# No plain pair of blocks in the first layer, the first half of tile 2's x kept only in sums, and other rules for the order of the work

## The chip, the cores and the metric

The kernel runs on one core of a Trainium2 chip: TensorE (PE) multiplies, VectorE (DVE), ScalarE (ACT) and GpSimd (POOL) do the elementwise work, SyncE (SP) issues the loads and stores. The metric is the device time of one execution in microseconds. Before the change the median of three runs is 571.93 (569.59 to 574.9).

## The reference

Linear attention with decay runs over 2 batches, 8 heads, 768 positions and 64 columns per head; its output, 1536 tokens of 512 columns, goes through two MLP layers of 2048 hidden columns.

```python
for b in range(nb):                        # blocks of 64 positions
    intra = einsum('bhic,bhjc->bhij', qb, kb) * Dmask
    out[:, :, sl] = einsum('bhij,bhjd->bhid', intra, vb) + einsum('bhid,bhde->bhie', qb * lam_pow, kv_state)
    kv_state = lam_block * kv_state + einsum('bhsd,bhse->bhde', kb * rev_pow, vb)
x = out.transpose(0, 2, 1, 3).reshape(1536, 512)
h = x @ w_in;  g = where(h > 0, h, exp(min(h, 0)) - 1);          x = g @ w_out      # layer 0
h = x @ w_in2; g = maximum(h, 0) + log1p(exp(-abs(h)));        out = g @ w_out2     # layer 1
```

## The kernel before

**Attention** goes in 12 chunks of 128 positions, 6 for each batch (`attention_ops`). A chunk has on PE the scores (tile `sps`, 16 small matmuls), the state (`stps`, not in the last chunk of a batch) and the mixing (`xps`: 16 matmuls with the state, L245, which the first chunk of a batch lacks, and 16 with the masked scores, L250). VectorE masks the scores (`sc`, L235), adds the state (L288), writes the low part of x (`xl`, L271). q is scaled by `qpow` (L211), k by `kdecay` (L219) and the state faded (L293) on POOL or VectorE. ScalarE writes the high part of x (`xh`, L267). q and k of a chunk come in one load (`qk`), k and v in another (`kv`), 512 KB each. From chunk 6 on `kv` has two buffers, so chunk 8's load waits for the mixing of chunk 6, and so on.

**The MLP.** Tokens form three tiles of 512 (t = 0, 1, 2; four chunks each), hidden columns 16 blocks of 128 for each layer. Each factor is kept as a high and a low part, so each 128 x 128 piece of a product takes three matmuls of 512 columns (L303 to L305). The first product of one tile and one block, x @ w_in (tile `hps`), has twelve; so has the second one, g @ w_out (tiles `y0` to `y3`, L353, a quarter each), which adds into `y` over four or more blocks. Between them stand ScalarE's and VectorE's activation and the split of g into two parts. Weights come packed (`raw`); two ScalarE passes, two VectorE passes, a ScalarE copy and a VectorE subtraction make the parts (`wih`, `wil`, `woh`, `wol`). There are two `raw` buffers, so a weight load waits until ScalarE has read the one before last.

**The plan** (`plan`) names the first products in order: `one` is tile 0 with one block; `two` is tiles 1 and 2 with a pair of blocks, four plain products of twelve matmuls (48); `fast` does the same pair with seven half products of six matmuls (42), from sums of x pieces (t1 to t4, `first_sums`) and sums of weight pieces (`sumsw`, `s0h` to `s1l`, `sum_ops`). With x11 and x12 for the first 256 columns of x in tiles 1 and 2, and x21 and x22 for the last 256, t1 = x12 - x11, t2 = x22 - t1, t3 = x22 - x12, t4 = x21 - t2. Before the change layer 0 has eight `one`, a `two`, three `fast`, and then groups of four `one` and two `fast`; layer 1 has only such groups.

**The order.** At build time `schedule` walks through the work with assumed durations and writes each engine's instructions into a fixed order, which the chip then follows; an engine waits where its next instruction isn't ready. An operation has a key (its due time) and those it waits for. For PE it chooses between attention, the next first product and the next second product: a second product is taken when no first product is ready, or when those that are ready pile up to `PILE` products (L444). POOL gets an operation only when VectorE has `QUEUE` of them ready. `FIRST_LOADS` sets the order of the first loads on SP.

Of the kernel before, what the change touches and what calls it, by code (L numbers as in the profile page):

```python
# [9 lines left out]
F32 = mybir.dt.float32  # L10
# [23 lines left out]
FAST = (True, True)  # L34

# [5 lines left out]
def plan():  # L41
    p = [("one", 0, c) for c in range(EARLY)]
    p += [("two", 0, 0)] + [("fast" if FAST[0] else "two", 0, q) for q in range(1, 4)]
    for b in (2, 3):
        p += [("one", 0, c) for c in range(4 * b, 4 * b + 4)]
        p += [("fast" if FAST[0] else "two", 0, q) for q in (2 * b, 2 * b + 1)]
    for b in range(4):
        p += [("one", 1, c) for c in range(4 * b, 4 * b + 4)]
        p += [("fast" if FAST[1] else "two", 1, q) for q in (2 * b, 2 * b + 1)]
    return p  # L50
# [5 lines left out]
def body(ctx, tc, lamc, attqk, attkv, w1, w2, out):  # L56
# [27 lines left out]
    def new_x(t, layer):  # L84
        for parts, k in ((xh, "h"), (xl, "l")):
# [170 lines left out]
    def att_parts(g):  # L256
# [134 lines left out]
    def schedule(pe, free):  # L391
# [8 lines left out]
        def enter(op):  # L400
            for e in op.on:
                if e != "P":
# [3 lines left out]
        def begin(op, e):  # L406
# [8 lines left out]
            if e == "S" and took[0] == "dma":  # L415
                wire[0] = max(now + LATENCY, wire[0]) + took[1]
# [4 lines left out]
            heappush(events, (now + late + 0.12, next(seen), op))  # L421
# [5 lines left out]
        while left:  # L427
# [11 lines left out]
            if free["P"] <= now:  # L439
# [4 lines left out]
                if can[0] and (not can[1] or sum(o.on["P"][0] for o in ahead) / (4 * MM3) >= PILE and not m1_seq[heads[1]].first):  # L444
# [29 lines left out]
    FIRST, STEP, ATT = 21.0, 7.0, 3.95  # L474
    SHIFT = 6
# [3 lines left out]
    FIRST_LOADS = [("q", 0), ("v", 0), ("q", 1), ("v", 1), ("q", 2), ("v", 2), ("q", 3), ("v", 3), 0, ("q", 4), ("v", 4), 1, ("q", 5), ("v", 5), ("q", 6)]  # L479
# [13 lines left out]
    def build():  # L493
# [22 lines left out]
        for kind, layer, c in PLAN:  # L516
# [3 lines left out]
            elif kind == "two":  # L520
                for i, t in PAIR:
                    stand((layer, t, 2 * c + i), 4 * MM3)
                    made[layer, t, 2 * c + i] = at_[0] + 4.0
# [28 lines left out]
        def weights_ops():  # L552
            for k, task in enumerate(tasks):
                key = want(task) - 3.0
# [3 lines left out]
                ld = Op({"S": ("dma", 1.28)}, lkey(k, key), w_load, [loads[t2][1] if t2 else None], lambda k=k: loaded[0] == k)  # L558
# [69 lines left out]
        att_seq, closed = [], []  # L628

        def attention_ops():  # L630
# [3 lines left out]
            ramp = Op({"V": (1.36, False)}, chunk_at(0) + 2.0, powers, [spin])  # L634
# [10 lines left out]
            for g in range(NCHUNK):  # L645
# [29 lines left out]
                O["SC", g, 0] = Op({"V": PS_V}, k + 1.2, lambda g=g: att_sc(g, 0), [s, spin, O.get(("X", g - 2))])  # L675
                O["SC", g, 1] = sc1 = Op({"V": PS_V}, k + 1.3, lambda g=g: att_sc(g, 1), [O["SC", g, 0]], end=gave(g))

                if not last:
# [9 lines left out]
                    if g % CPB < CPB - 2:  # L688
                        O["FD", g] = Either(F_ON, k + 2.5, lambda e, g=g: att_fade(e, g), [ad, O.get(("AD", g - 1)), ramp])
# [7 lines left out]
                homes = []  # L697
# [651 lines left out]
```

## Time and profile before

| | us |
|---|---|
| median of 3 runs | 571.93 |
| the profiled execution | 572.88 |
| its span, first to last instruction | 571.2 |
| PE busy in the span | 555.7 |
| VectorE busy | 497.8 |
| ScalarE busy | 390.4 |
| POOL busy | 14.4 |

The span is what the trace covers; the profiled execution's own time has 1.7 us more. A row of a timeline gives when an instruction starts, how long it takes and, in brackets, how long its engine had been idle and what ended that. Durations of neighbours overlap a little (an operation on VectorE of 0.68 is followed by the next after 0.60), so prices are read from start to start. The granted clock is TensorE's, as a share of its full 2.4 GHz.

### The profile page before, as it was taken

Reading aid. Unit: us, or ns where it says so; the run is one execution under the profiler, and the core shown is the slowest. Engines: PE = TensorE matmul, PEld = TensorE weight load, DVE = VectorE, ACT = ScalarE, POOL = GpSimd, SP = SyncE. Lnnn points to the kernel's source line nnn. Section 1 sums busy time; section 2 is a strip of 40 time slices with the busy share of each in tenths; the row PEclk is TensorE's granted clock in tenths of the full one; section 3 lists DMA queues with packets and bytes.
Section 4 is the critical chain, followed back from the end, with each engine's and each line's share of the span. In section 5 each row is a group of like instructions: output and inputs, shape, how many; then the busy total and the mean of one; then the engine's idle time right before and its main releaser. Section 6 shows DMA issues by size and latency. Waiting matters only on the chain.

```text
span 571.2 us, 7940 instructions
## 1 busy us (share of the span) xinstructions
PE 555.7 (97%) x2933; PEld 458.0 (80%) x2933; DVE 497.8 (87%) x883; ACT 390.4 (68%) x699; POOL 14.4 (3%) x18
## 2 busy tenths in 40 slices
PE   8798899999999999999999999999999999999997
PEld 7687678888887888888888887888888888888885
DVE  7988789998958499876898999999999999986883
ACT  1376558566765678635878669997999678965550
POOL 1201210000000000000000000000000000000000
PEclk9899799999999999999999999999999999999999
DMA  8955643002014033300233001221122321000023
GB/s 318 405 199 189 242 162 112 0 1 73 2 46 140 26 111 113 127 30 1 73 111 111 1 1 38 73 75 55 56 75 75 109 72 42 1 0 0 2 92 130
DMA packets 14583, 49.80 MB, mean 87 GB/s; under 512 B 1745, under 2 KB 1745, under 8 KB 14545
## 3 DMA queue, kind: packets, MB, share of 16 engines
q1 hardware_dynamic: 14544, 49.30, 25.2%
q8 instruction: 23, 0.38, 0.3%
q14 instruction: 16, 0.12, 0.1%
HBM read 46.14 MB, written 3.15 MB: 86 GB/s over the span
## 4 chain that ended last, share of the span: by engine, by line
PE 89%; DMA 5%; DVE 3%; SPq 1%; ACT 1%; issue 1%; POOL 0%; POOLq 0%; DVEq 0%; ACTq 0%
PE y L353 44%; PE hps L303 6%; PE hps L304 6%; PE hps L305 6%; PE pa L304 5%; PE pa L303 5%; PE pa L305 5%; DMA raw<-w 3%; PE pd L303 2%; PE pd L304 2%; PE pd L305 2%; DMA kv<-attkv 2%; PE xps L250 2%; PE xps L245 1%; PE pb L303 1%; PE pb L304 1%
## 5 line engine op out<-in xcount | busy, mean ns | idle before, releaser
L353 PE MATMUL y<-woh,g 128*128 128x512 f32 x384 | 118.7, 390 | 1.1 <-DVE g L485 0.7
L353 PE MATMUL y<-g,woh 128*128 128x512 f32 x384 | 118.8, 390 | 0.0
L802 ACT ACTIVATE g<-v 128x512 fp32r<-128x512 f32 x96 | 60.4, 629 | 52.2 <-PE y L353 47.6
L485 DVE TENSOR_TENSOR g<-v,g 128x512 fp32r<-128x512 f32 x96 | 65.7, 686 | 22.7 <-ACT g L802 22.2
L353 PEld LDWEIGHTS y<-woh,g 128*128 128x128 f32 x384 | 72.1, 188 | 16.7 <-DVE g L485 1.0
L353 PEld LDWEIGHTS y<-g,woh 128*128 128x128 f32 x384 | 71.8, 188 | 15.2
L353 PE MATMUL y<-g,wol 128*128 128x512 f32 x192 | 74.7, 389 | 0.0
L353 PE MATMUL y<-wol,g 128*128 128x512 f32 x192 | 74.7, 389 | 0.0
L303 PE MATMUL hps<-xh,wih 128*128 128x512 f32 x136 | 53.7, 395 | 1.8 <-DVE xl2b L271 1.1
L304 PE MATMUL hps<-xl,wih 128*128 128x512 f32 x136 | 53.2, 391 | 0.0
L305 PE MATMUL hps<-xh,wil 128*128 128x512 f32 x136 | 53.0, 390 | 0.0
L564 ACT ACTIVATE r<-raw 128x512 f32<-128x512 f32 x64 | 42.7, 668 | 13.9 <-DMA raw<-w 9.3
L1121 DVE TENSOR_TENSOR yacc<-y,yacc 128x512 f32<-128x512 f32 x68 | 45.4, 688 | 5.8 <-PE y L353 5.4
L578 DVE CUSTOM_DVE_ANT_0 r<-r,c 128x1024 uint16<-128x1024 uint16 x64 | 45.2, 707 | 2.0 <-ACT c L568 1.0
L568 ACT ACTIVATE c<-raw 128x512 uint32<-128x512 uint32 x64 | 42.4, 663 | 0.1
L353 PEld LDWEIGHTS y<-g,wol 128*128 128x128 f32 x192 | 36.0, 188 | 7.5
L353 PEld LDWEIGHTS y<-wol,g 128*128 128x128 f32 x192 | 36.0, 188 | 7.5
L783 DVE SCALAR_TENSOR_TENSOR u<-u,e 128x512 f32<-128x512 f32 x48 | 32.8, 685 | 5.0 <-ACT v L779 5.0
L485 DVE TENSOR_TENSOR v<-v,u 128x512 f32<-128x512 f32 x48 | 32.9, 685 | 0.2
L303 PEld LDWEIGHTS hps<-xh,wih 128*128 128x128 f32 x136 | 25.7, 189 | 8.0 <-issue 1.4
L573 DVE TENSOR_SCALAR r<-r 128x512 uint32<-128x512 uint32 x64 | 27.3, 427 | 5.3 <-ACT r L564 5.3
L363 ACT ACTIVATE e<-e 128x512 f32<-128x512 f32 x48 | 30.0, 624 | 0.4
(187 smaller groups left out, 1103.9 us busy)
## 6 DMA issues: line engine op xcount, KB each, us to landing
raw<-w SPq DMA_DIRECT2D x64, 512.0 KB, 3.7
qk<-attqk SPq DMA_DIRECT2D x8, 512.0 KB, 7.1
kv<-attkv SPq DMA_DIRECT2D x8, 512.0 KB, 5.5
out<-yacc SPq DMA_DIRECT2D x12, 256.0 KB, 2.1
early<-attkv SPq DMA_DIRECT2D x2, 512.0 KB, 9.4
early<-attqk SPq DMA_DIRECT2D x2, 512.0 KB, 10.8
earlykv<-attkv SPq DMA_DIRECT2D x2, 512.0 KB, 11.2
earlyqk<-attqk SPq DMA_DIRECT2D x2, 512.0 KB, 11.1
```

What stands on the lines that cost most here:

```text
L303: T.matmul(ps, wh[:, wo[i]], xa[i], start=(start and i == 0), stop=False, skip_group_check=True)
L304: T.matmul(ps, wh[:, wo[i]], xb[i], start=False, stop=False, skip_group_check=True)
L305: T.matmul(ps, wl[:, wo[i]], xa[i], start=False, stop=(stop and i == n - 1), skip_group_check=True)
L353: T.matmul(yps[m], a, b, start=(begins(key) and i == 0), stop=(ends(key) and i == 2))
L363: A.activation(out=o, in_=a, func=AF.Exp, scale=-1.0)
L485: engines[e].tensor_tensor(out=o, in0=a, in1=b, op=ALU.subtract)
L564: A.activation(out=r, in_=high.bitcast(F32), func=AF.Prelu, scale=2.0 ** -112, alpha=-2.0 ** 32)
L568: A.activation(out=box["c"], in_=box["low"], func=AF.Copy, scale=2.0 ** -29)
L578: V.tensor_tensor(out=ri, in0=ri, in1=box["c"], op=ALU.add)
L783: V.scalar_tensor_tensor(out=u, in0=u, scalar=-1.0, in1=box["e"], op0=ALU.add, op1=ALU.subtract)
L802: A.activation(out=g[:, 0], in_=box["v"], func=AF.Copy)
L1121: V.tensor_tensor(out=y, in0=yps[m], in1=y, op=ALU.add)
```

## The change

The pair of blocks 0 and 1 of layer 0 becomes `fast` like the others. With it the split form of x12 has no user but the sums: the split tiles of tile 2 hold only the last 256 columns of x, and `att_copy` writes the mixing's result of chunks 8 to 11 once more as fp32 into a tile that lies in the place of `yacc0` (`x2`). `first_sums` works on that copy in place: t3 = x22 - x12 first, then t1, t2 and t4, with 12 adds for 20, and with no wait for the end of attention except for t3's parts.

In `schedule` second products are held during attention (`HELD`, 7.9 products, until attention's buffers are closed), after it they pile up to 2.4; POOL takes work when VectorE has two operations ready; weights get a due time 0.16 ahead of their use where it was 3.0; a load is assumed to land later (`LATE`) and results to be seen sooner (`MARGIN`); chunks 6 and 7 use the early PSUM banks (`SHIFT`); for chunks 0 to 7 q is scaled on VectorE alone; the keys of the attention steps and the order of the first loads are others (q 2, q 3, then v 2, v 3, q 4, and two weights ahead of v 4).

```diff
 def plan():
     p = [("one", 0, c) for c in range(EARLY)]
-    p += [("two", 0, 0)] + [("fast" if FAST[0] else "two", 0, q) for q in range(1, 4)]
+    p += [("fast", 0, q) for q in range(4)]
...
 def new_x(t, layer):
...
-                parts[t] = [
-                    None if layer and FAST[1] and i == "a" else
-                    xp.tile([P, 2, TT], F32R, tag=f"x{k}2{i}", name=f"x{k}2{i}") for i in "ab"
-                ]
+                parts[t] = None, xp.tile([P, 2, TT], F32R, tag=f"x{k}2b", name=f"x{k}2b")
...
 def att_parts(g):
-        return [(xps[g][:, 2 * i:2 * i + 2], xh[t][i][:, :, o], xl[t][i][:, :, o]) for i in range(2)]
+        return [(xps[g][:, 2:4], xh[t][1][:, :, o], xl[t][1][:, :, o])]
...
+    def att_copy(g, y):
+        o = slice(g % 4 * P, g % 4 * P + P)
+        A.activation(out=y[:, :, o], in_=xps[g], func=AF.Copy)
...
 def schedule(pe, free):
...
-                if can[0] and (not can[1] or sum(o.on["P"][0] for o in ahead) / (4 * MM3) >= PILE and not m1_seq[heads[1]].first):
+                if can[0] and (not can[1] or sum(o.on["P"][0] for o in ahead) / (4 * MM3) >= (PILE if late else HELD) and not m1_seq[heads[1]].first):
...
-    PILE, QUEUE = 1.9, 3
+    PILE, HELD, QUEUE = 2.4, 7.9, 2
...
+    KT, LATE, RAW_LAG, MARGIN = 3.0, 3.42, 0.28, 0.05
...
-                key = want(task) - 3.0
+                key = want(task) - KW
...
+                    O["XC", g] = Op({"A": SCALAR}, k + KX, copy, [xh_, O.get(("XC", g - 1))])
...
-        def first_sums(plain_end):
+        def first_sums():
...
+            box = held["x2"]
+            made = [attend["XC", g] for g in range(8, NCHUNK)]
...
+            def sub(key, fn, out_, a, b, deps):
+                return Either(T_SUM, key, lambda e: fn(e, out_(), a(), b()), deps)
...
+            def y(n, k):
+                return box["x2"][:, 2 * n + k]
...
             for k in range(2):
-                t1 = chain(("f1", k), at_[1], [start_],
-                           (minus, lambda k=k: x(2, 0, k)[0], lambda k=k: x(1, 0, k)[0]),
-                           (plus, None, lambda k=k: x(2, 0, k)[1]),
-                           (minus, None, lambda k=k: x(1, 0, k)[1]))
...
+                def new3(e, k=k):
+                    if "f3" not in box:
+                        box["f3"] = xp.tile([P, 2, TT], F32, tag="xh2a", name="f3")
+                    minus(e, box["f3"][:, k], y(1, k), y(0, k))
+
+                ya, yb, fc = lambda k=k: y(0, k), lambda k=k: y(1, k), lambda k=k: box["f3"][:, k]
+                f3 = Either(T_SUM, at_[3] - 3.0, new3, made + early_q)
+                f1 = sub(at_[1], minus, ya, ya, lambda k=k: x(1, 0, k, 0), [f3] + x1)
+                f1 = sub(at_[1], minus, ya, ya, lambda k=k: x(1, 0, k, 1), [f1])
+                f2 = sub(at_[2], minus, yb, yb, ya, [f1])
...
+                f4 = sub(at_[4], minus, ya, lambda k=k: x(1, 1, k, 0), yb, [f2, l1])
+                f4 = sub(at_[4], plus, ya, ya, lambda k=k: x(1, 1, k, 1), [f4])
...
-            elif kind == "two":
-                first = not any(k == "two" and l == layer and x < c for k, l, x in PLAN)
...
```


What this moves is seen at three places of the order.

**Place 1: VectorE at start-up**, up to the low part of chunk 3's x, on which the first MLP product waits (`sc`: masked scores, `r`, `c` and `wil`: a weight's conversion, `kv`, `early`: a k that is scaled or a q). Before:

```order
L485 TENSOR_TENSOR wil0_351<-r_301,wih0_328 128x512
L235 TENSOR_TENSOR sc_367<-sps0_313,dmask_96 128x512
L288 TENSOR_TENSOR state_371<-stps_330,faded_308 128x256
L235 TENSOR_TENSOR sc_367<-sps1_314,dmask_96 128x512
L235 TENSOR_TENSOR sc_376<-sps0_341,dmask_96 128x512
L573 TENSOR_SCALAR r_353<-r_353 128x512
L235 TENSOR_TENSOR sc_376<-sps1_342,dmask_96 128x512
L578 ISA r_353<-r_353,c_355 128x1024
L219 TENSOR_TENSOR kv_224<-kv_224,kdecay_97 128x512
L288 TENSOR_TENSOR state_418<-stps_357,faded_374 128x256
L485 TENSOR_TENSOR wil1_421<-r_353,wih1_416 128x512
L271 TENSOR_TENSOR xl0_227<-xps_378,xh0_226 128x4x128
```

Now:

```order
L287 TENSOR_TENSOR state_295<-stps_270,faded_264 128x256
L230 TENSOR_TENSOR sc_314<-sps0_282,dmask_96 128x512
L206 TENSOR_TENSOR early_139<-early_139,qpow_98 128x512
L230 TENSOR_TENSOR sc_314<-sps1_283,dmask_96 128x512
L574 TENSOR_SCALAR r_316<-r_316 128x512
L574 TENSOR_SCALAR r_324<-r_324 128x512
L579 ISA r_316<-r_316,c_321 128x1024
L270 TENSOR_TENSOR xl0_212<-xps_297,xh0_211 128x4x128
L287 TENSOR_TENSOR state_364<-stps_328,faded_318 128x256
L490 TENSOR_TENSOR wil0_368<-r_316,wih0_362 128x512
L579 ISA r_324<-r_324,c_366 128x1024
L270 TENSOR_TENSOR xl0_212<-xps_342,xh0_211 128x4x128
```

Ahead of the fourth `xl` stand the masked scores of chunks 0 to 3 now and of 0 to 4 before; two weights are converted together, and the scalings of two k's have left VectorE.

**Place 2: SP and PE in the middle of attention.** On SP (`kv_609`, `kv_696` and now `kv_569`, `kv_663` are the k and v of chunks 8 and 9). Before:

```order
L138 DMA raw_476<-w1 128x512
L138 DMA raw_509<-w1 128x512
L138 DMA raw_541<-w1 128x512
L138 DMA raw_579<-w1 128x512
L206 DMA kv_609<-attkv 128x1024
L138 DMA raw_634<-w1 128x512
L138 DMA raw_692<-w1 128x512
L206 DMA kv_696<-attkv 128x1024
L196 DMA qk_701<-attqk 128x1024
```

Now:

```order
L133 DMA raw_497<-w1 128x512
L133 DMA raw_523<-w1 128x512
L201 DMA kv_569<-attkv 128x1024
L133 DMA raw_600<-w1 128x512
L201 DMA kv_663<-attkv 128x1024
L191 DMA qk_668<-attqk 128x1024
L133 DMA raw_670<-w1 128x512
L191 DMA qk_686<-attqk 128x1024
L201 DMA kv_704<-attkv 128x1024
```

On PE, from the mixing of chunk 7 to the state of chunk 9 (`stps_752`, now `stps_742`). Before:

```order
L245 MATMUL xps_650<-qk_239,state_591 64x128 x8
L250 MATMUL xps_650<-sc_628,kv_278 64x128 x8
L303 MATMUL hps_679<-xh0_226,wih2_483 128x512
...
L229 MATMUL sps0_710<-qk_299 128x128
...
L280 MATMUL stps_727<-kv_609 64x64 x8
L280 MATMUL stps_752<-kv_696 64x64 x8
```

Now:

```order
L240 MATMUL xps_619<-qk_215,state_550 64x128 x8
L245 MATMUL xps_619<-sc_598,kv_279 64x128 x8
L240 MATMUL xps_646<-qk_292,state_615 64x128 x8
L245 MATMUL xps_646<-sc_617,kv_569 64x128 x8
L279 MATMUL stps_676<-kv_569 64x64 x8
L224 MATMUL sps0_692<-qk_340 128x128
...
L352 MATMUL y2_715<-g0_473,woh0_548 128x512 x2
...
L302 MATMUL hps_722<-xh0_211,wih2_515 128x512
...
L279 MATMUL stps_742<-kv_663 64x64 x8
```

Chunk 9's load has one weight load between it and chunk 8's, where it had two; between the mixing of chunk 7 and the state of chunk 9 PE now has the mixing of chunk 8, its state, the scores of chunk 9 (`sps0_692`), a quarter of a second product and a first product.

**Place 3: VectorE ahead of the first `fast` pair**, around the sums (`sumsw`: of weights; `sums`, `x2`: of tokens; `t1l` to `t3l`, `s0l`: low parts). Before:

```order
L485 TENSOR_TENSOR sums_1111<-xh2b_811,sums_1111 128x512
L488 TENSOR_TENSOR sumsw_1143<-sumsw_1143 128x256
L488 TENSOR_TENSOR sums_1111<-sums_1111,xl2b_813 128x512
L485 TENSOR_TENSOR sums_1111<-xh2b_811,sums_1111 128x512
L485 TENSOR_TENSOR sumsw_1143<-sumsw_1143 128x256
L485 TENSOR_TENSOR g1_1206<-v1_1163,g1_1206 128x512
L485 TENSOR_TENSOR sumsw_1143<-sumsw_1143 128x256
L485 TENSOR_TENSOR t2l_1210<-sums_1111,t2h_1209 128x512
L488 TENSOR_TENSOR sums_1111<-sums_1111,xl2b_813 128x512
L485 TENSOR_TENSOR s0l_1231<-sumsw_1143,s0h_1216 128x512
L485 TENSOR_TENSOR sumsw_1143<-sumsw_1143 128x256
L485 TENSOR_TENSOR sums3_1112<-xh2b_811,xh2a_810 128x512
```

Now:

```order
L490 TENSOR_TENSOR x2_702<-x2_702,xh1_475 128x512
L493 TENSOR_TENSOR sumsw_1064<-sumsw_1064 128x256
L490 TENSOR_TENSOR x2_702<-x2_702,xl1_476 128x512
L490 TENSOR_TENSOR x2_702<-x2_702 128x512 x2
L490 TENSOR_TENSOR t1l_1086<-x2_702,t1h_1085 128x512
L490 TENSOR_TENSOR t2l_1185<-x2_702,t2h_1184 128x512
L490 TENSOR_TENSOR g1_1200<-v0_1131,g1_1200 128x512
...
L490 TENSOR_TENSOR sumsw_1064<-sumsw_1064 128x256
L490 TENSOR_TENSOR t3l_1041<-f3_998,t3h_1040 128x512
...
L490 TENSOR_TENSOR sumsw_1064<-sumsw_1064 128x256
L490 TENSOR_TENSOR s0l_1225<-sumsw_1064,s0h_1222 128x512
```

Each token sum takes one operation where high and low parts were added one by one; the second weight pair's conversions and activations of the `one` blocks stand among them on both sides. On PE, four first products, four and a quarter second products and the pair's first two half products now stand between the mixing of chunk 11 and the pair's third half product, the first that needs the sums.

## Rows read from the trace of the kernel before

**Rows 1.** The page: busy tenths and granted clock in 40 slices; shares of the chain.
```profile
PE   8798899999999999999999999999999999999997
...
PEclk9899799999999999999999999999999999999999
...
PE 89%; DMA 5%; DVE 3%; SPq 1%; ACT 1%; issue 1%; POOL 0%; POOLq 0%; DVEq 0%; ACTq 0%
```
**Rows 2.** Stages from the span's start: length, busy us of each engine, clock, DMA.
```profile
0.00:4.83 4.83, 3.71 (x15) 3.28 (x16) 2.91 (x9) 1.28 (x1) 0.70 (x6) 1.00 0.53 176
4.83:30.70 25.87, 21.39 (x321) 18.33 (x320) 23.58 (x44) 6.61 (x11) 5.43 (x5) 0.93 1.02 400
30.70:98.60 67.90, 62.99 (x542) 50.54 (x541) 57.66 (x105) 45.24 (x82) 8.31 (x7) 0.95 0.53 177
98.60:126.00 27.40, 27.40 (x122) 22.71 (x121) 27.04 (x50) 16.40 (x29) 0.00 (x0) 1.00 0.00 1
126.00:567.50 441.50, 440.20 (x1938) 363.10 (x1936) 386.04 (x679) 320.85 (x577) 0.00 (x0) 1.00 0.18 58
```
**Rows 3.** The chain, undisturbed places: start, us, engine, tile, line, instructions.
```profile
...
38.48 1.09 PE sps L229 x16
...
42.52 0.61 PE stps L280 x16
...
71.66 1.02 PE xps L245 x16
72.68 1.05 PE xps L250 x16
...
98.76 8.16 PE y L353 x36
...
```
**Rows 4.** Timeline of PE, start-up: start, us, line, tiles, idle before and releaser.
```profile
4.83 2.08 PE L229 MATMUL sps<-qk 64*128 64x128 f32 x16
...
30.70 0.50 PE L303 MATMUL hps<-xh,wih 128*128 128x512 f32 x1
```
**Rows 5.** Timeline of PE in the middle of attention.
```profile
55.40 0.69 PE L280 MATMUL stps<-kv 128*64 128x64 f32 x16
...
64.10 0.80 PE L303 MATMUL hps<-xh,wih 128*128 128x512 f32 x1
...
67.55 1.16 PE L229 MATMUL sps<-qk 64*128 64x128 f32 x16
```
**Rows 6.** The chain through that place.
```profile
52.64 5.34 DMA kv<-attkv
58.15 1.05 POOL kv L219
59.24 1.12 PE stps L280 x16
60.36 1.90 PE xps L245 x16
```
**Rows 7.** Timeline of SP, the queue that issues all loads, there.
```profile
46.65 5.89 SPq L138 DMA_DIRECT2D raw<-w  x2
```
**Rows 8.** The chain on VectorE: a long and a short operation, start to start.
```profile
22.27 0.60 DVE wil L485
...
23.48 0.34 DVE state L288
```
**Rows 9.** Timeline of VectorE: start, us, line, operation, tiles.
```profile
19.90 1.77 DVE L219 TENSOR_TENSOR earlykv<-earlykv,kdecay 128x512 f32<-128x512 f32 x1
...
28.26 0.69 DVE L271 TENSOR_TENSOR xl<-xps,xh 128x512 fp32r<-128x512 f32 x1 [0.19 <-ACT xh L267]
...
104.34 0.69 DVE L485 TENSOR_TENSOR s0l<-sumsw,s0h 128x512 fp32r<-128x512 f32 x1
```
**Rows 10.** What VectorE waited for up to 99 us: total us, times, longest.
```profile
DVE kv L219 <- DMA kv<-attkv: 4.1, 3, 1.6
```
**Rows 11.** Timeline of POOL at that place.
```profile
19.87 1.26 POOL L211 TENSOR_TENSOR early<-early,qpow 128x512 f32<-128x512 f32 x1 [0.43 <-PE sps L229]
```

More of the change, by code (lines that the diff above doesn't have):

```diff
@@ L401, in enter @@
             for e in op.on:
-                if e != "P":
+                if e == "D":
+                    op.gone = True
+                    heappush(events, (now + op.on[e], next(seen), op))
+                elif e != "P":
                     ready[e].append((op.key, op.n, op))
@@ L415, in begin @@
             if e == "S" and took[0] == "dma":
-                wire[0] = max(now + LATENCY, wire[0]) + took[1]
+                wire[0] = max(now + (LATENCY if now < 5.0 else LATE), wire[0]) + took[1]
                 took = 0.46, wire[0] - now
@@ L420, in begin @@
             heappush(events, (free[e], next(seen), None))
-            heappush(events, (now + late + 0.12, next(seen), op))
+            heappush(events, (now + late + MARGIN, next(seen), op))
         for op in ops:
@@ L624, in give_bank @@
             banks[owner[id(ps)]] = True
-        att_seq, closed = [], []
+        att_seq, closed, held = [], [], {}
         def attention_ops():
@@ L688, in attention_ops @@
                     if g % CPB < CPB - 2:
[L689 removed]
+                        O["FD", g] = Either(F_ON if g > EASY else F_EARLY, k + KF, lambda e, g=g: att_fade(e, g), [ad, O.get(("AD", g - 1)), ramp])
+                if not first:
+                    O["QP", g] = Either(Q_ON if g > EASY else Q_EARLY, k + KQ, lambda e, g=g: att_prep(e, g), [s, ramp])
                 def mix(g=g):
@@ L848, in plain @@
             return parts[-1]
-        held = {}
         sums = {}
@@ new lines, in first_sums, with x @@
+            box = held["x2"]
+            made = [attend["XC", g] for g in range(8, NCHUNK)]
+            x1 = [attend["XL", g] for g in range(4, 8)]
+            early_q = [attend[n] for n in (("KP", 2), ("ST", 2), ("X", 2), ("S", 3), ("X", 3))]
+            t1_home = [attend[n] for g in (4, 5, 6) for n in (("KP", g), ("S", g), ("ST", g), ("X", g)) if n in attend]
+            def x(t, h, k, part):
+                return f32((xh, xl)[part][t][h][:, k])
+            def y(n, k):
+                return box["x2"][:, 2 * n + k]
@@ L1079, in first_sums @@
+            for h in hi4:
+                h.behind(*f3s)
+            held["acc", 0] = done[2] + done[4]
             tdone[0] = done
@@ L1126, in unit_ops @@
                     deps += held.get(("acc", t), []) + mine[:1]
-                    if layer == 0 and t == 1:
-                        deps += held.get("sums", [])
                     if layer == 0 and t == 2:
@@ L1245, in close_units @@
                 if t in ysplit and (1, t) not in xdone:
-                    if t == 0 or not FAST[1]:
+                    if t == 0:
                         split_ops(t)
@@ L1256, in build @@
                 keys_done.add((layer, 0, c))
-            elif kind == "two":
-                first = not any(k == "two" and l == layer and x < c for k, l, x in PLAN)
-                for i, t in PAIR:
-                    o = plain(layer, t, 2 * c + i, layer == 1 and first and i == PAIR_FIRST[t])
-                    xuse[t] = [o]
-                    plain_end[t] = o
-                    keys_done.add((layer, t, 2 * c + i))
-                gone["i", layer * NF + 2 * c] = gone["i", layer * NF + 2 * c + 1] = o
-            else:
-                if layer == 0 and 0 not in tdone:
-                    first_sums(plain_end.get(2))
+            else:
                 o = quick(layer, c)
```

111 lines of the change are left out of this document (40 added, 71 removed).

## The prediction

> **What bounds the kernel now.** All sums stand against the profiled execution: 572.88 us, of which the span is 571.2. The median of the three timed runs, 571.93, lies 0.95 under it, and that is taken off at the end. I take 1% (5.7 us) as what a measurement of this kernel can tell from no change.
>
> I read the slices of the page first. PE's digits are below 9 in four of the first five slices (71 us) and then only in the last, the granted clock dips in the second and the fifth, and the chain that ended last is 89% PE [rows 1]. The table of stages says the same in microseconds: from 98.60 to 567.5 PE lacks 1.3 us in all, and VectorE, at 27.04 of 27.40 us, is as full as PE just behind attention [rows 2]. So the time is PE's work plus what PE loses in the first 98.6 us.
>
> The work is priced from the undisturbed chain [rows 3]. 36 matmuls of 512 columns take 8.16 us: 0.227 each, 2.72 for the twelve of one product. One chunk of attention is scores 1.09, state 0.61, mixing 1.02 + 1.05 = 2.07 (1.03 without a state).
>
> - Up to the first MLP product, at 30.70, PE did six scores, five states, mixing 0 to 4: 6.54 + 3.05 + 1.03 + 8.28 = 18.9 us, from a start at 4.83 [rows 4]. It lost 30.70 - 4.83 - 18.9 = **7.0 us**.
> - From 30.70 to 98.60 it did nine first products and four second ones (35.4), six scores (6.54), five states (3.05), mixing 5 to 11 (13.45): 58.4 of 67.9 us. It lost **9.5 us**.
>
> The second loss has one large place. The state of chunk 8 starts at 55.40 and ends about 0.61 later; that of chunk 9, next on PE, starts at 59.24 [rows 5, 6]: 3.2 us of nothing. Behind it the clock is at its lower level, 1.2 GHz for 2.4 (the dip of the fifth slice): the state takes 1.12 for 0.61, the mixing's first half 1.90 for 1.02, and the product that follows 67.55 - 64.10 = 3.45 for 2.72. From 59.24 to 67.55 that is 8.31 us for 0.61 + 2.07 + 2.72 = 5.40, so 2.9. Together **6.1 us**. The cause stands in the chain [rows 6] and in SP's queue [rows 7]: the k and v of chunk 9 is issued only at 52.64, because two weight loads stand ahead of it from 46.65 on and wait for ScalarE; it takes 5.34 to land, then POOL scales k in 1.05.
>
> **The change part by part.**
>
> *The plain pair.* Four products of twelve matmuls (48) become seven of six (42). Six matmuls go: 6 x 0.227 = **-1.4**, PE being full wherever they stood. This term has no other end.
>
> *Sums and halves.* The token sums of this layer take 12 VectorE adds for 20, and four low halves of x go: 8 x 0.60 + 4 x 0.34 = 6.2 us less of VectorE [rows 8]. ScalarE gains four copies and loses four halves, about 1 us; it is busy 45 of 68 us [rows 2], so that costs nothing. VectorE's 6.2 us count only where PE waits for it, below.
>
> *Start-up.* The first product waits for the low part of chunk 3's x, done at 28.95 [rows 9]. Ahead of it, and with it, VectorE has 26 long operations and 8 short ones before, 23 and 4 now (the order, place 1; the scans at the start are the same). That is 3 x 0.60 + 4 x 0.34 = 3.2 us earlier, so 25.8. The weights now land one load later (the order of the loads), in a place where VectorE still works on scores. By 25.8 PE has done six scores, five states and mixing 0 to 3, 16.8 us; it lost 25.8 - 4.83 - 16.8 = 4.2 for 7.0. Mixing 4 and 5 follow behind the product. Gain **-2.8**; ends 0 (POOL, which now also scales k there, slows VectorE as at 19.90, where one operation took 1.77 us [rows 9]) and -6 (only the slow first score, 2.08 for 1.09, stays).
>
> *Middle.* The k and v of chunk 9 stands behind one weight load in place of two, which waits for the weight conversion of two tasks before (place 2); I take it as issued when mixing 7 ends. From there to the state of chunk 9, PE had a product, scores 8 and state 8: 2.72 + 1.09 + 0.61 = 4.4 us of cover. Now mixing 8, state 8, scores 9, a quarter of a second product (0.68) and a first product stand there: 2.07 + 0.61 + 1.09 + 0.68 + 2.72 = 7.2. The load and the scaling need 5.34 + 0.60 on VectorE, where this k is now scaled: 5.9. So the wait goes, and with it the slow clock: **-6.1**. What is late next is the load for chunk 8, behind mixing 6: its cover is scores 7, state 7, scores 8, two quarters, mixing 7 and 8, 8.3 us against 5.34 + 1.05 on POOL. Chunks 10 and 11 have 12 and more. Ends: -9.5 (no loss at all), and 0 where another load takes its place.
>
> *Given back.* Second products 4 to 8 now stand behind attention, and the pair's third half product needs its token and weight sums. PE's work up to it: 4.83, attention 42 (12 x 1.09 + 10 x 0.61 + 2 x 1.03 + 10 x 2.07), eight first products 21.8, seven and a quarter second ones 19.7, the pair's first two half products 2.7: 91.0; with the losses left (4.2 + 9.5 - 6.1 = 7.6) PE is there at 98.6. VectorE: up to the low half of the first weight sum, at 105.03 [rows 9], it was busy 2.91 + 23.58 + 57.66 + 6.43 = 90.6 [rows 2]. Counted in the order, 123 long and 22 short operations stand there now for 124 and 28: 0.60 + 6 x 0.34 = 2.6 less, 88.0. It idled 98.6 - 84.2 = 14.4 us before, 4.1 of them waiting for k and v [rows 10]. Without these 10.3 is left: 98.3. PE and VectorE arrive together, so I book **+1.0**; ends 0 and +7 (VectorE idles as before, 102.4, and a wait of 3.8 brings the slow clock's 2.9).
>
> Sum: -1.4 - 2.8 - 6.1 + 1.0 = -9.3; 572.88 - 9.3 - 0.95 = **562.6 us**.
>
> The rest of the order, 100 to 567 us, is much alike, and VectorE has 55 us of air there [rows 2]; I cost it at nothing. Without that cover, one lost weight conversion is a wait of a few microseconds.
>
> Two things speak against the change. POOL does 15 tensor operations for 12, five of them scalings of k for two; beside POOL's at 19.87 [rows 11] VectorE's at 19.90 took 1.77 us, where such a one is followed by the next after 0.60 [rows 8, 9]. The Trainium skill, GPSIMD Engine Reference, section Key points, says that GpSimd shares its SBUF interfaces with VectorE and contends with its two-input operations; the trace agrees with that 1.77, and by it VectorE would need some 3 x 1.1 = 3.3 us more, which the first rival takes in. And holding second products back takes filler out of attention: five first and four second products stood ahead of the end of mixing 11, four and three do now, 5.4 us less. The Trainium skill, Perfetto Trace Analysis, section Optimization Strategy, advises to interleave stages whose limits differ; place 2 speaks against that here, since the cover that is left lies behind each load. Where it holds, the second rival comes.
>
> **The rivals.**
>
> *VectorE sets the end of attention* (12%). For it: 27.04 of 27.40 us busy from 98.60 on, and more POOL work beside it. It idles its 14.4 us again, the pair's third half product waits until 102.4, and the slow clock adds 2.9: PE loses 102.4 + 2.9 - 91.0 = 14.3 for 16.5. With -1.4: 572.88 - 2.2 - 1.4 - 0.95 = **568.3**.
>
> *The filler is missing* (7%). The two products less in attention come back as waits for masked scores and states: 5.4 us. Against it: the forecast's cover at each load. -9.3 + 5.4 = -3.9, so **568.0**.
>
> *Only the plain pair counts* (4%): the new rules move waits without ending them. 572.88 - 1.4 - 0.95 = **570.5**.
>
> *The k and v loads wait at every chunk, slower* (7%). Loads of chunks 8 to 11 need a buffer that the mixing two chunks before sets free. If a load takes over 7.2 us with its scaling (queued behind a weight load, or SP held by ScalarE), each of the four states waits 3.2 and slows the clock by 2.9, with 5.4 us less filler between. It decides from three such waits on: 18.3 - 6.1 - 1.4 - 2.8 = +8.0, so **580**. Against it: one such wait in four before.
>
> *Better than forecast* (10%): PE's losses end near 5 us, only start-up. -1.4 - (16.5 - 5) = -12.9, so **559**.
>
> **How the numbers follow.** The forecast has 60%, its own range 558 to 567. Range 556 to 570: it holds the forecast, the better case and the rivals at 568, and leaves out the slower one, the one at 570.5 and the edges. Faster by over 1% (under 566.2) is the forecast but for its upper edge, with the better case: 0.67; within 1% the three middle rivals and that edge: 0.26; slower 0.07.
>
> **What would show it.** The first product starts near 26 and not 30.7; no state waits 3 us, and the clock stays up between 45 and 70; mixing 11 ends near 70 to 74 for 87; the first pair's third half product near 98 without a wait; from there a full PE. A wait of over 3 us ahead of that product is the first rival, waits of states the slower one. The prediction is wrong where PE loses more than 12 us before 100, or any at all behind it.

## The result and the profile after

The changed kernel takes **557.8 us** (median of four runs, 557.2 to 558.53), against 572.2 (569.59 to 574.9) beside it: ratio 0.9748, 95% interval 0.9701 to 0.9796. The profiled execution took 557.2 us, its span is 555.5. It is 14.4 us faster where 9.3 was forecast, inside the range and 4.8 us below the forecast number.

The page of the changed kernel: busy tenths of PE, the granted clock and the chain of waits, which answer to [rows 1].

```profile
PE   8999999999999999999999999999999999999997
...
PEclk9999999999999999999999999999999999999999
...
PE 92%; DMA 5%; DVE 1%; SPq 0%; ACT 0%; issue 0%
```

Three of the four thin slices are gone, and both dips of the clock. The stages, cut at the first product (24.19) and at the pair's third half product (94.92), answer to [rows 2] (length, then busy us of PE, PEld, DVE, ACT, POOL, then the clock, the DMA share and GB/s):

```profile
4.83:24.19 19.36, 17.90 (x290) 15.26 (x289) 17.46 (x35) 5.91 (x10) 5.64 (x6) 1.00 1.02 400
24.19:94.92 70.73, 70.43 (x612) 57.51 (x612) 66.48 (x120) 48.95 (x91) 10.66 (x9) 1.00 0.57 199
94.92:126.00 31.08, 31.08 (x139) 25.75 (x138) 30.74 (x60) 21.84 (x39) 0.00 (x0) 1.00 0.05 17
126.00:548.00 422.00, 422.00 (x1862) 349.11 (x1861) 373.74 (x657) 313.16 (x563) 0.00 (x0) 1.00 0.18 60
```

PE lacks 0.30 us in the 70.73 up to the pair's third half product. The list of PE's waits from the first product on (us, times, longest) is two lines long in the changed kernel:

```profile
PE hps L302 <- DVE xl L270: 0.4, 1, 0.4
PE stps L279 <- DVE v L365: 0.3, 1, 0.3
```

and in the kernel before it had the long wait of [rows 5, 6] and four more:

```profile
PE stps L280 <- POOL kv L219: 3.2, 1, 3.2
PE hps L303 <- DVE xl2b L271: 1.1, 1, 1.1
PE y L353 <- DVE g L485: 0.7, 1, 0.7
PE hps L303 <- DVE state L288: 0.6, 1, 0.6
PE y L353 <- ACT g L802: 0.4, 1, 0.4
```

The places of [rows 4, 5] on PE's timeline now: first product, mixing of chunk 7, state of chunk 9 (without a wait, and at 0.69 us for 1.12), third half product.

```profile
24.19 0.50 PE L302 MATMUL hps<-xh,wih 128*128 128x512 f32 x1 [0.41 <-DVE xl L270]
...
41.49 1.09 PE L240 MATMUL xps<-qk,state 64*64 64x128 f32 x16
42.51 1.09 PE L245 MATMUL xps<-sc,kv 128*64 128x128 f32 x16
...
50.77 0.69 PE L279 MATMUL stps<-kv 128*64 128x64 f32 x16
...
94.92 0.39 PE L302 MATMUL pd<-t1h,s0h 128*128 128x512 f32 x1
```

VectorE's `s0l`, the last thing that half product needs from it, answers to the last row of [rows 9] (it was 104.34):

```profile
93.57 0.69 DVE L490 TENSOR_TENSOR s0l<-sumsw,s0h 128x512 fp32r<-128x512 f32 x1
```

It ends at 94.26, 0.66 us ahead of PE.

At start-up the kernel before had two waits on PE that [rows 4] leave out:

```profile
22.33 0.69 PE L280 MATMUL stps<-earlykv 128*64 128x64 f32 x16 [2.58 <-DVE xl L271]
23.95 1.73 PE L245 MATMUL xps<-early,state 64*64 64x128 f32 x16 [0.94 <-DVE state L288]
```

VectorE's low part of chunk 3's x, for which the first product waits, starts at 23.45 now (28.26 in [rows 9]). Ahead of it some operations of VectorE were stretched, two before besides the 1.77 of [rows 9], and two now (like ones take 0.42 for 128x256 and 0.68 for the others):

```profile
14.09 0.98 DVE L293 TENSOR_TENSOR faded<-state,qpow 128x256 f32<-128x256 f32 x1
18.29 1.69 DVE L578 CUSTOM_DVE_ANT_0 r<-r,c 128x1024 uint16<-128x1024 uint16 x1
```
```profile
14.69 0.93 DVE L206 TENSOR_TENSOR qk<-qk,qpow 128x512 f32<-128x512 f32 x1
22.41 1.12 DVE L579 CUSTOM_DVE_ANT_0 r<-r,c 128x1024 uint16<-128x1024 uint16 x1
23.45 0.68 DVE L270 TENSOR_TENSOR xl<-xps,xh 128x512 fp32r<-128x512 f32 x1
```

**Where the time came from.** Cutting each profile into the same stretches, PE's idle time is length minus busy time, and what the lower clock may cost is (1 - clock) x length, since at 1.2 GHz PE's work takes nearly twice as long (half a mixing 1.90 us for 1.02 in the kernel before). Both are worked out from tables like that of the stages, cut at 30, 60, 126, 340 and 360, in us; the three stretches of the kernel before that lose most:

```profile
0.00:30.00 30.00, 24.40 (x325) 21.03 (x327) 26.15 (x51) 7.57 (x12) 6.13 (x11) 0.94 0.94 364
30.00:60.00 30.00, 26.20 (x264) 21.03 (x264) 26.30 (x46) 20.68 (x36) 4.18 (x4) 0.97 0.60 204
60.00:126.00 66.00, 64.89 (x417) 52.81 (x414) 58.74 (x109) 41.30 (x76) 4.13 (x4) 0.96 0.28 94
```

| kernel | idle 0-30 | 30-60 | 60-126 | 340-360 | clock | sum | span |
|---|---|---|---|---|---|---|---|
| before | 5.6 | 3.8 | 1.1 | 1.1 | 5.3 | 16.9 | 571.2 |
| changed | 2.6 | 0.3 | 0 | 0 | 0 | 2.9 | 555.5 |

The difference of the sums is 14.0; with 1.4 for the six matmuls 15.4, of 15.7 in the spans. So the account closes: 8.7 us are idle time of PE, 5.3 the lower clock, 1.4 matmuls.

### The profile page after: what moved, and what is told of

The parts are those of the page before. It is cut to its first block, busy times and chain, and to the rows that moved or that the text cites. A ratio compares the mean times of both kernels' runs of the same rounds, so it can differ in the third digit from the quotient of the medians.

```text
span 555.5 us, 7918 instructions
## 1 busy us (share of the span) xinstructions
PE 548.8 (99%) x2927; PEld 453.6 (82%) x2927; DVE 494.2 (89%) x882; ACT 391.1 (70%) x702; POOL 17.0 (3%) x21
## 3 DMA queue, kind: packets, MB, share of 16 engines
q1 hardware_dynamic: 14544, 49.30, 25.8%
HBM read 46.14 MB, written 3.15 MB: 89 GB/s over the span
## 4 chain that ended last, share of the span: by engine, by line
PE 92%; DMA 5%; DVE 1%; SPq 0%; ACT 0%; issue 0%
PE y L352 47%; PE pa L303 5%; PE pa L304 5%; PE pa L302 5%; PE hps L302 5%; PE hps L304 5%; PE hps L303 5%; PE pd L302 3%; PE pd L304 3%; PE pd L303 3%; DMA earlyqk<-attqk 2%; DMA raw<-w 2%; DMA early<-attqk 1%; PE pb L303 1%; PE pb L304 1%; PE pb L302 1%
## 5 line engine op out<-in xcount | busy, mean ns | idle before, releaser
L352 PEld LDWEIGHTS y<-woh,g 128*128 128x128 f32 x384 | 72.1, 188 | 15.1
L302 PE MATMUL hps<-xh,wih 128*128 128x512 f32 x128 | 50.1, 392 | 0.4 <-DVE xl L270 0.4
L304 PE MATMUL hps<-xh,wil 128*128 128x512 f32 x128 | 49.8, 389 | 0.0
L303 PE MATMUL hps<-xl,wih 128*128 128x512 f32 x128 | 49.8, 389 | 0.0
L362 ACT ACTIVATE v<-v 128x512 f32<-128x512 f32 x48 | 30.0, 624 | 0.4
```

What stands on the lines that cost most here:

```text
L302: T.matmul(ps, wh[:, wo[i]], xa[i], start=(start and i == 0), stop=False, skip_group_check=True)
L303: T.matmul(ps, wh[:, wo[i]], xb[i], start=False, stop=False, skip_group_check=True)
L304: T.matmul(ps, wl[:, wo[i]], xa[i], start=False, stop=(stop and i == n - 1), skip_group_check=True)
L352: T.matmul(yps[m], a, b, start=(begins(key) and i == 0), stop=(ends(key) and i == 2))
L362: A.activation(out=o, in_=a, func=AF.Exp, scale=-1.0)
```

## The experiments

Every experiment's profile fits the same account (the five columns plus 552.6 us of other time, or 554.0 with the plain pair, give the span within 1.0 us, but for the two runs with extra VectorE work, within 1.7). The experiments ran on three chips, and the changed kernel's 557.8 was not taken again beside them. At a granted clock of 1.0 the kernel before took 566.95 and 567.24 us on one chip, 567.57 and 567.92 on another, so a difference of under 1 us tells nothing.

| kernel | idle 0-30 | 30-60 | 60-126 | 340-360 | clock | span | median of runs |
|---|---|---|---|---|---|---|---|
| structure alone | 5.4 | 3.3 | 1.0 | 1.1 | 5.0 | 568.8 | 570.6 |
| rules alone | 3.0 | 0 | 1.5 | 0 | 0 | 558.9 | 562.0 |
| before, load ahead of one weight | 7.0 | 1.0 | 1.6 | 1.1 | 1.8 | 565.9 | 568.4 |
| before, spacing alone | 4.9 | 1.3 | 2.2 | 1.1 | 1.8 | 566.1 | 568.3 |
| changed, load behind two weights | 3.1 | 0.2 | 0 | 0 | 0 | 555.6 | 557.4 |
| changed, load behind three | 3.8 | 0 | 1.1 | 0 | 0 | 557.3 | 559.2 |
| changed, spacing undone | 2.6 | 0.5 | 5.5 | 0 | 2.0 | 564.2 | 565.9 |
| changed, POOL's share undone | 4.1 | 2.4 | 0.4 | 0 | 0 | 559.7 | 560.8 |
| changed, old order of first loads | 3.3 | 0.2 | 0 | 0 | 0 | 556.1 | 557.8 |
| changed, old due time of weights | 2.0 | 0.6 | 0 | 0 | 0 | 555.9 | 557.6 |
| changed, six t3 more, planned | 3.9 | 0 | 2.5 | 0 | 0 | 560.1 | 560.9 |
| changed, six t3 more, not planned | 2.4 | 0.6 | 2.6 | 0 | 0 | 559.9 | 561.1 |

**Structure or rules?** The change has two halves that can be built apart. The structure with the old rules:

```diff
-    PILE, HELD, QUEUE = 2.4, 7.9, 2
-    FIRST, STEP, ATT = 22.11, 5.28, 3.95
+    PILE, HELD, QUEUE = 1.9, 1.9, 3
+    FIRST, STEP, ATT = 21.0, 7.0, 3.95
...
-    KT, LATE, RAW_LAG, MARGIN = 3.0, 3.42, 0.28, 0.05
+    KT, LATE, RAW_LAG, MARGIN = 3.0, 2.15, 0.0, 0.12
...
```

> The changed structure (blocks 0 and 1 as seven half products, token sums from the fp32 copies in 12 adds) with the old constants and keys of the order. Its loads stand as before: two weight loads ahead of chunk 9's k and v; VectorE has the same 44 long and 8 short operations up to chunk 3's low part of x as before. Theory (the gain is waits that the new rules end in the first 98.6 us): first product still near 30, chunk 9's state still waits 3 us or more, and only the six matmuls go: 572.2 - 1.4 = 570 to 571. Rival (the structure does it, 6.2 us less of VectorE let PE run on): 560 to 565, without the wait at chunk 9.

Measured: 570.6 us (568.79 to 573.63), ratio to before 1.0008 (0.9978 to 1.0039). Its four longest waits from 20 to 110 us, on PE's timeline:

```profile
21.98 0.69 PE L279 MATMUL stps<-earlykv 128*64 128x64 f32 x16 [2.59 <-DVE xl L270]
23.61 1.97 PE L240 MATMUL xps<-early,state 64*64 64x128 f32 x16 [0.94 <-DVE state L287]
...
58.41 1.12 PE L279 MATMUL stps<-kv 128*64 128x64 f32 x16 [3.07 <-POOL kv L214]
...
81.59 0.50 PE L302 MATMUL hps<-xh,wih 128*128 128x512 f32 x1 [0.97 <-DVE xl2b L270]
```

Start-up and chunk 9 wait as before, the rival that VectorE's 6.2 us would free PE falls. The six matmuls don't show in the medians. Among executions with a mean granted clock of 0.991 on the same chip they seem to (570.1 to 570.7 here, 571.4 to 572.8 of the kernel before), but not at 0.997 (568.97 against 568.45 and 569.02). So no run prices them; the 1.4 rests on their count (PE has 2927 matmuls for 2933) and on 0.227 each. The other half, the old structure with the new rules:

```diff
-    PILE, QUEUE = 1.9, 3
-    FIRST, STEP, ATT = 21.0, 7.0, 3.95
+    PILE, HELD, QUEUE = 2.4, 7.9, 2
+    FIRST, STEP, ATT = 22.11, 5.28, 3.95
...
+    KT, LATE, RAW_LAG, MARGIN = 3.0, 3.42, 0.28, 0.05
...
```

> The old structure (blocks 0 and 1 as a plain pair of 48 matmuls, 20 adds) with the new constants, keys and order of loads; one weight load ahead of chunk 9's k and v. Theory: first product near 24 to 25, no wait at chunk 9, nearly all of the gain but the six matmuls: 557.8 + 1.4 = 559, up to 562 if the 6.2 us more of VectorE make PE wait ahead of the first pair that needs token sums. Rival (structure): 568 or more.

Measured: 562.0 us (560.64 to 564.03), ratio 0.9862 (0.9811 to 0.9913). Start-up and the middle are nearly as in the changed kernel (3.0 us idle for 2.6, and 0 for 0.3). The profile's span is 3.4 us longer than the changed kernel's: 1.4 for the six matmuls, and a wait at the product between the mixings of chunks 10 and 11:

```profile
66.68 0.47 PE L303 MATMUL hps<-xh,wih 128*128 128x512 f32 x1 [1.52 <-DVE xl2b L271]
```

The median is 4.2 longer, as two of the four executions, at a granted clock of 0.997 and 0.996, took 563.21 and 564.03. The kernel before has that wait too (1.1 us), and so has the structure alone (0.97, the last of its rows); only both halves together end it. So the rules carry the gain, and that one wait needs the structure with them.

**The place of chunk 9's load.** The forecast put the long wait down to the two weight loads ahead of that load. In the kernel before, one of them was put behind it:

```diff
-                ld = Op({"S": ("dma", 1.28)}, lkey(k, key), w_load, [loads[t2][1] if t2 else None], lambda k=k: loaded[0] == k)
+                ld = Op({"S": ("dma", 1.28)}, lkey(k, key), w_load, [loads[t2][1] if t2 else None], lambda k=k: loaded[0] == k and (k != 9 or attend["LV", 9].gone))
```

> The kernel before with one thing other: the tenth weight load waits until chunk 9's k and v are issued, so one weight load stands ahead of it and not two. The order up to there is the same, start-up too; behind it the order of PE and VectorE is worked out anew. Theory: the load is issued when mixing 7 ends and not at 52.64, chunk 9's state waits under 1 us and the clock stays up from 59 to 68: 572.2 - 6.1 = 566 (567.5 if the later weight makes a wait of its own, 563 if it also ends later ones). Rival (a load that comes earlier only moves the wait to the next load or to masked scores): 571 to 573.

Measured: 568.4 us (567.18 to 571.75), ratio 0.9983 (0.9953 to 1.0014): no difference that is measured. SP's queue and the state of chunk 9:

```profile
51.04 0.33 SPq L206 DMA_DIRECT2D kv<-attkv  x1
```
```profile
49.90 1.09 PE L250 MATMUL xps<-sc,kv 128*64 128x128 f32 x16
...
56.76 0.69 PE L280 MATMUL stps<-kv 128*64 128x64 f32 x16 [0.82 <-DVE state L288]
```

The load is issued as mixing 7 ends, at 51.04 for 52.64. In the kernel before mixing 7 ended at 50.71, so the two weight loads had cost 1.9 us. The wait shrank to 0.82 and the clock stayed up behind it, as expected; but the profile has 1.4 us more idle at start-up, with the same order there, and 0.5 more ahead of a later product. The converse, on the changed kernel:

```diff
-                    get(("KP", old_v), ("ST", old_v), ("X", old_v)), lambda g=g: g in at)
+                    get(("KP", old_v), ("ST", old_v), ("X", old_v)), lambda g=g: g in at and (g != 9 or loaded[0] > 7))
```

> The changed kernel with one thing other: chunk 9's k and v are issued only behind one weight load more, as two of them stood ahead before. Theory: that weight load waits for ScalarE, chunk 9's state waits some 2 to 4 us and the clock falls for a few us behind it: 557.8 + 3 to 6 = 561 to 564. Rival (cover in the new order hides it): 557 to 559.

Measured: 557.4 us (557.29 to 558.26). The theory misses. SP's queue:

```profile
43.83 0.33 SPq L133 DMA_DIRECT2D raw<-w  x1
44.25 0.38 SPq L201 DMA_DIRECT2D kv<-attkv  x1
```

The weight load ahead is issued at 43.83, when ScalarE has read the buffer that it needs (the read of `raw` into `c`, from 43.13 on). The mixing of chunk 7, which the load of chunk 9 needs anyway, ends at 43.6, so the weight load costs 0.6 us (44.25 for 43.64). In the changed kernel ScalarE's read has the same place, its row here:

```profile
43.13 0.66 ACT L569 ACTIVATE c<-raw 128x512 uint32<-128x512 uint32 x1
```

In the kernel before, ScalarE waited 3.11 us for VectorE (the bracket of the first row) and came to that read only at 51.54:

```profile
51.00 0.63 ACT L583 ACTIVATE woh<-r 128x512 fp32r<-128x512 f32 x1 [3.11 <-DVE r L578]
51.54 0.66 ACT L568 ACTIVATE c<-raw 128x512 uint32<-128x512 uint32 x1
```

ScalarE waited for a pass of VectorE (`r`, L578), and VectorE had itself waited, one operation ahead of that pass, for the load of chunk 8:

```profile
49.67 0.69 DVE L219 TENSOR_TENSOR kv<-kv,kdecay 128x512 f32<-128x512 f32 x1 [1.55 <-DMA kv<-attkv]
```

So what a weight load ahead cost here, 1.9 or 0.6 us, went by how late its buffer was read. One weight load more, so that it goes behind three:

```diff
-                    get(("KP", old_v), ("ST", old_v), ("X", old_v)), lambda g=g: g in at)
+                    get(("KP", old_v), ("ST", old_v), ("X", old_v)), lambda g=g: g in at and (g != 9 or loaded[0] > 8))
```

> The changed kernel with chunk 9's k and v issued behind three weight loads and chunk 10's q and k, so some 10 us later (near 54 for 43.64). The order puts three more quarters of a second product and no first product ahead of that state. Theory (a k and v that comes late is felt, since only 5 to 8 us of PE work can stand in its place): a wait of 2 to 5 us near 55 to 60 with the lower clock behind it, 561 to 566. Rival (the second products that are held back fill the hole): 557.5 to 559.

Measured: 559.2 us (558.45 to 559.75), near the rival. The load is issued at 48.52, not 54, and nothing waits for it: PE does scores and first and second products up to mixing 9 at 55.83, and the states of chunks 9 and 10 run together at 57.78; from 30 to 60 it has no idle time at all. In this profile start-up idles 1.2 us more than in the changed kernel's, and 60 to 126 1.1 more.

**The spacing of attention.** `STEP` sets when each chunk is due.

```diff
-    FIRST, STEP, ATT = 22.11, 5.28, 3.95
+    FIRST, STEP, ATT = 22.11, 7.0, 3.95
```

> The changed kernel with chunks of attention due every 7.0 us, as before, and not every 5.28. Two weight loads stand ahead of chunk 9's k and v again, and first and second products stand between chunks as before. Theory (what ended the wait at chunk 9 is attention packed densely behind the first products): a wait of 1 to 3 us at a state between 45 and 65, 560 to 564. Rival (the assumed lateness of loads and the earlier weights hide it whatever the spacing): 557.5 to 558.5.

Measured: 565.9 us (565.25 to 566.46), ratio 0.9897 (0.983 to 0.9963), 8.1 more than the changed kernel. The price is above the theory's, and the place is another: no state waits more than 0.5 us from 30 us on, though two weight loads stand ahead of chunk 9's load; PE waits for VectorE ahead of mixing 9 and 10, and longest at a first product behind mixing 10.

```profile
61.97 1.09 PE L240 MATMUL xps<-qk,state 64*64 64x128 f32 x16 [0.83 <-DVE v L365]
...
69.65 1.09 PE L240 MATMUL xps<-qk,state 64*64 64x128 f32 x16 [0.67 <-DVE xl2b L270]
...
77.14 0.79 PE L302 MATMUL hps<-xh,wih 128*128 128x512 f32 x1 [3.87 <-DVE xl2b L270]
```

That product reads `xh` and `wih`, not `xl2b`. I take it that it waits for the PSUM bank that `xl2b` frees by reading `xps`; no run tried that by itself. The same constants alone (`FIRST` 22.11, `STEP` 5.28) in the kernel before:

```diff
-    FIRST, STEP, ATT = 21.0, 7.0, 3.95
+    FIRST, STEP, ATT = 22.11, 5.28, 3.95
```

> The kernel before with only the spacing of the chunks of attention changed, due every 5.28 us and the first product at 22.11, for 7.0 and 21.0; one weight load stands ahead of chunk 9's k and v. Start-up is the same up to the fourth state. Theory (dense chunks end the wait at chunk 9, start-up keeps its 7 us): 566 to 567. Rival (dense chunks without the other rules come too soon for their loads and wait at several states): 571 to 576.

Measured: 568.3 us (567.87 to 569.03), ratio 0.994 (0.9911 to 0.9969): 4.0 us of the 14.4 by the medians, 1.8 to 5.1 by the interval. The long wait at chunk 9 is gone, start-up isn't (5 us idle, the clock at 0.94), and waits of 0.4 to 1.5 stand between 56 and 68. Neither theory nor rival: spacing is needed for the gain and is a small part of it alone. The long wait at chunk 9 ends with the spacing alone, and it also stays away with the other rules and the old spacing; which of the two ends it in the changed kernel no run tells.

**POOL's share at start-up.** POOL gets an operation only when VectorE has three ready, as before:

```diff
-    PILE, HELD, QUEUE = 2.4, 7.9, 2
+    PILE, HELD, QUEUE = 2.4, 7.9, 3
```

> The changed kernel where POOL takes an operation only when VectorE has three ready, as before, and not two; VectorE then has 43 long and 8 short operations up to chunk 3's low part of x, for 41 and 4. Theory (POOL's scalings of k are what ends the 2.6 us that PE waits for chunk 3's state at start-up): that wait comes back, with the lower clock behind it in some executions: 560 to 564. Rival (start-up is ended by the other rules): 557.5 to 559.

Measured: 560.8 us (559.79 to 561.54), 3.0 more than the changed kernel. The size is the theory's, the place isn't: chunk 3's state waits 0.55, not 2.6, so another of the rules ends most of that wait, and which one no run isolates. PE waits for VectorE's scalings of q, and later for a low part of x:

```profile
12.38 1.09 PE L240 MATMUL xps<-qk,state 64*64 64x128 f32 x16 [0.31 <-DVE qk L206]
15.79 1.09 PE L240 MATMUL xps<-qk,state 64*64 64x128 f32 x16 [0.79 <-DVE qk L206]
21.26 0.69 PE L279 MATMUL stps<-earlykv 128*64 128x64 f32 x16 [0.55 <-POOL earlykv L214]
...
59.55 0.49 PE L224 MATMUL sps<-qk 64*128 64x128 f32 x2 [1.93 <-DVE xl2b L270]
```

**The order of the first loads**, as before, in the changed kernel:

```diff
-    FIRST_LOADS = [..., ("q", 2), ("q", 3), ("v", 2), ("v", 3), ("q", 4), 1, 0, ("v", 4), ("q", 5), ("q", 6), ("v", 5)]
+    FIRST_LOADS = [..., ("q", 2), ("v", 2), ("q", 3), ("v", 3), 0, ("q", 4), ("v", 4), 1, ("q", 5), ("v", 5), ("q", 6)]
```

> The changed kernel with the old order of the first loads (k and v 2 ahead of q and k 3, one weight load ahead of q and k 4). VectorE has 44 long and 6 short operations up to chunk 3's low part of x, for 41 and 4. Theory (VectorE's count of operations sets the first product): 3 x 0.60 + 2 x 0.34 = 2.5 us later, near 26.7, and the time 560. Rival (what ends PE's waits at start-up is the order of VectorE's work, not its count): first product near 24 to 25, 557.5 to 558.5.

Measured: 557.8 us (557.75 to 558.32). The first product starts at 26.66, just as the count of VectorE's operations says, and the time is unchanged: PE does scores, states and mixing in those 2.5 us instead. **The first product's start is not the loss.**

**The due time of the weights:**

```diff
-    KQ, KK, KF, KS, KX, KW, KL = 1.98, 0.2, 2.5, 1.24, 3.32, 0.16, 12.0
+    KQ, KK, KF, KS, KX, KW, KL = 1.98, 0.2, 2.5, 1.24, 3.32, 3.0, 12.0
```

> The changed kernel with the weights' due time 3.0 ahead of their use, as before, and not 0.16. Theory (with it weight conversions stand ahead of activations, which made PE wait 1.1 us near 343 to 353 in every kernel with the old rules): that wait comes back, and VectorE is later at start-up, since conversions go ahead of masked scores: 559 to 562. Rival (the due time does nothing that is felt): 557.5 to 558.5.

Measured: 557.6 us (557.45 to 557.92): the rival. PE's wait near 343 to 353, which every kernel with the old rules has (1.1 in the table) and none with the new, has another cause; which rule ends it stays open.

**Do VectorE and PE arrive together?** t3 was written more often than needed, which changes no value:

```diff
+                for _ in range(EXTRA):
+                    f3 = Either(T_SUM, at_[3] - 3.0, new3, [f3])
```

> The changed kernel with t3 written three more times for each half of its columns: six more VectorE operations, 6 x 0.60 = 3.6 us, ahead of the token sums; the order is otherwise word for word the same. Theory (VectorE and PE arrive nearly together at the first pair's third half product: 0.66 us between the end of s0l, 94.26, and PE, 94.92): a wait of 3.6 - 0.66 = 2.9 us there, 557.8 + 2.9 = 560.7, up to 564 if the clock falls behind it. Rival (VectorE has air, its work was done long before): 557.5 to 558.5.

Measured: 560.9 us (560.38 to 561.77). The price fits, but the place doesn't: the planner saw the extra work and put two quarters of a second product more ahead of the pair's third half product, and PE starts that one at 97.27 without a wait. PE waits behind it (1.17 us at 104.72, 0.94 at 121.72), and start-up idles 1.3 us more than in the changed kernel's profile. So the same six operations were written inside the one that writes t3, which the planner doesn't see:

```diff
-                    minus(e, box["f3"][:, k], y(1, k), y(0, k))
+                    for _ in range(4):
+                        minus(e, box["f3"][:, k], y(1, k), y(0, k))
```

> As the run with six more VectorE operations, but written where t3 is written anyway, so that the planner doesn't see them: each engine's order is word for word that of the changed kernel, with two t3 written four times. (In that earlier run, which named its order unchanged, PE got two quarters of a second product more ahead of the pair's third half product.) Theory (VectorE and PE arrive together there): PE waits 3.6 - 0.66 = 2.9 us at that half product, 560.7, 564 if the clock falls behind it. Rival (VectorE had air there; the earlier run lost its 3 us elsewhere): 557.5 to 558.5.

Measured: 561.1 us (560.61 to 561.96): 3.3 for 3.6 us of VectorE. Three of PE's waits, all between 78 and 99 us:

```profile
PE hps L304 <- DVE wil L490: 1.0, 1, 1.0
PE pd L302 <- ACT s0h L906: 1.0, 1, 1.0
...
PE hps L302 <- ACT wih L584: 0.5, 1, 0.5
```

They sum to 2.5 us, of which 1.0 lies at the third half product itself (98.44 for 94.92) and 1.5 at a weight's conversion before it, near 79 to 81. VectorE has next to no air from there to that product.

## Why the prediction was right, and too small

The direction, the bound and the mechanism held: PE was the bound, its losses in the first 98.6 us were the thing to win, and they are won. What came is the case called "better than forecast" (10%): PE's losses up to the pair's third half product, by the prediction's own working, are 94.92 - 91.0 = 3.9 us for 16.5. By its steps:

- *Plain pair, -1.4*: fits the account above, whose error is up to 1.0 us; six matmuls are gone, and no run prices them alone.
- *Start-up, -2.8 forecast*: with the first product at 24.19 and the same 16.8 us of work ahead of it, PE lost 24.19 - 4.83 - 16.8 = 2.6 for 7.0, so **-4.4**. The term was sized from the event (VectorE 3.2 us earlier, 25.8). The old order of loads moved that event by 2.5 us and the time by nothing. The loss itself was two waits (2.58 and 0.94) and the clock at 0.93 [rows 2] behind them, and both go. The gain lies midway between the chosen value and the bound "only the slow first score stays" (-6). The count of VectorE's operations missed that the stretched ones would be fewer: ahead of chunk 3's low part of x they cost 2.7 us before and 0.7 now, and VectorE came 4.8 us earlier (24.13 for 28.95) for the 3.2 of the count. More POOL work did not slow VectorE more: from 4.83 to 72, six of its operations took over 0.15 us longer than their like on both sides, 4.3 us in all before and 2.8 now.
- *Middle, -6.1 forecast*: 0.3 us idle from 24.19 to 94.92, and by the same working 1.3 lost for 9.5, so **-8.2**. The named wait and the clock behind it did end. Of the 3.4 us that the step left standing 1.8 were two waits (0.65 for a state, 1.11 for `xl2b`) that the forecast hadn't listed and kept without a reason. Its cause was half right: the two weight loads had cost 1.9 us of the 3.15, and one load more ahead costs nothing in the new order (557.4). What ended the long wait isn't one rule: dense spacing alone ends it in the kernel before, the other rules end it without the spacing, and undoing the spacing gives 8.1 us back at other places.
- *Given back, +1.0 forecast, 0 measured*: PE came at 94.92 for 98.6 and `s0l` ended at 94.26 for 98.3. Both moved by some 4 us, and "arrive together" held: 0.66 us of air by the trace, and 3.6 us more on VectorE cost 3.3, of which 1.0 at that product.
- *Rest at nothing*: 1.1 us of waiting near 343 to 353 went as well, unforeseen.

The terms as measured sum to -15.1, of 15.7 between the two profiled spans.

The first rival (VectorE sets the end of attention) is not what came, but it is what stands next: each of four edits that give VectorE work (rules alone, less its six matmuls; POOL's share; both t3 runs) costs 2.8 to 3.3 us, though at different places. The second (filler missing) leaned on the hold of second products, and that does nothing here: with `HELD` at 2.4 or 1.9 each engine's order is word for word the same. From the first product on no state waits for a load, so the slower rival has nothing.

## What to carry to other kernels

Price the loss, not an event: PE's idle time plus (1 - clock) x length by stretch closes the account within 1 us in most profiles here, while the first product's start, in the run with the old order of loads, moved by 2.5 us for nothing. When a change re-plans a stretch, list every wait in it and say of each why it stays; those kept without a reason went. And a load's place in a queue matters only where the load ahead of it waits: read first when that one's buffer comes free.

## What the runs showed of the hardware

The clock makes the kernel before spread. In 39 of its executions beside these experiments, the four with a mean granted clock of 1.0 took 566.95 to 567.92 us, the twelve at 0.994 to 0.997 took 568.45 to 571.23, the 23 below took 571.19 to 575.74; the changed kernel's four are at 1.0 and lie within 1.4 us. So the same program has the lower clock in some executions and less of it in others, and 4 to 5 of the 14.4 us is that; whether the waits differed there no trace shows. Waits of 2 to 4 us on PE had the lower clock behind them in several profiles (3.15 before, 3.87 with the spacing undone). The seven of 0.2 to 1.9 us with POOL's share undone had none (1.00 throughout), but with the spacing alone two of 1.28 and 1.42 at start-up had it (0.94 up to 30 us), so the length of a wait alone doesn't tell.

PE's idle time in the first 30 us of one order differs by 1.2 to 1.4 us between profiles (5.6 and 7.0 for the order before, 2.6 and 3.8 for the new one), so a difference of that size at start-up needs more than one profile.
